# First batch of a channel-attention and FFN kernel: k loaded ahead of q, finer last parts of q, v transposed between the folds

## The chip, the cores and the metric

The kernel runs on one core of a Trainium2 chip. The metric is device time in microseconds, the median of several runs: 580.56 us for the kernel before, in 6 runs from 580.22 to 581.6. The engines are named as in the profile: PE is TensorE (PEld its weight loads), DVE VectorE, ACT ScalarE, POOL GpSimd, SP SyncE.

## The reference

q, k and v have the shape (4, 5824, 256) in float32: four batches of 5824 tokens with 256 channels. Attention is across channels, so its score matrix is 256 x 256 per batch, and its output goes through a feed-forward block with a product of two branches (d_ff = 1024):

```python
qn = q / (np.linalg.norm(q, axis=1, keepdims=True) + 1e-06)
kn = k / (np.linalg.norm(k, axis=1, keepdims=True) + 1e-06)
s = kn.transpose(0, 2, 1) @ qn / tau
a = np.exp(s - s.max(-1, keepdims=True))
a /= a.sum(-1, keepdims=True) + 1e-09
x = (v @ a).reshape(B * N, C)
out = ((x @ w1) * (x @ w2)) @ w3 @ w_out
```

tau is 1.0.

## The kernel before, in words

The attention matrix of a batch is folded into the weights: Wf = a @ [w1 w2] (256 x 2048), so that the tokens of v go directly to the two branches; w3 @ w_out is multiplied out once, into W_sb. The main loop (`emit_ab`, `emit_out`) then runs over 12 chunks of 512 tokens per batch and 8 blocks of 128 hidden channels: four 512-column matmuls of Wf against transposed v (line 419), ScalarE copies branch a (425), VectorE multiplies with branch b (428), and four 256-column matmuls with W_sb add to the output (452). While batch b is in its main loop, batch b+1's scores are computed in between, by a list with due times (`make_agenda`).

For batch 0 there is no earlier main loop to hide in. Its scores, softmax and folds are written out by hand, in program order, in lines 484 to 556; each engine takes its instructions in this order. A batch has 45 full tiles of 128 tokens and 64 tokens left over. They are loaded in six pieces, five of eight tiles and one (piece 5) of five tiles and the leftover. A piece of eight tiles is 512 KB in SBUF, one tile 64 KB; the loads convert float32 to bfloat16 and are all issued from POOL's queue, in program order (`load_piece`, lines 108 to 118, `cuts` splits a piece into several transfers). Buffers: five for q, so q's piece 5 takes the buffer of its piece 0, six for k, three for v.

What TensorE does with each tile of batch 0:

- `squares` (line 221): two 128-column matmuls that add the tile's squared columns into PSUM (`sqk` for k, `sqq` for q). The diagonal gives the norms.
- `products` (line 233), for q tiles, with the k tile of the same index: two 256-column matmuls that add to the score matrix G.
- `busy(n)` (line 209): n filler matmuls of 512 columns with no use for the result.

Issue order of the loads before: k0 (two halves), q0 (two halves), then k1 q1 k2 q2 k3 q3 k4 k5, q4 (two halves), q5 (leftover, then parts of two, two and one tiles), then w1 and w2 (first halves), half of v's piece 0, the second halves of w1, w2 and v's piece 0, v1, w3, w_out, v2. TensorE's order: squares of k0, then q0, then for pieces 1 to 3 squares of k, two fillers, squares and products of q; then squares of k4 and k5, k's norms, q4, q5.

The steps of the softmax (`soft_units`): `k_first` takes the diagonal of the k squares (DVE, 244); `k_row` spreads it by a float32 matmul (272) and makes 1/norm in four ScalarE activations (274 to 277); `q_first` (251) takes q's diagonal; `scaled_first` scales G (302), makes q's 1/norm (291 to 294) and the exponentials e, two on ScalarE (307); `first_folds` makes the column sums (323), 1/sum (329, 330) and folds 0 to 5. A fold is two 512-column matmuls (344) and an eviction to Wf, scaled by 1/sum, on ScalarE for even folds (351) and on VectorE for odd ones (353). Folds 6 and 7 come within the main loop. Before `first_folds` (line 555), TensorE transposes the first four tiles of v, 8 matmuls (132), and VectorE copies them out (136). The main loop's first matmul needs folds 0 and 1 and this part of v, its third folds 2 and 3.

Of the kernel before, what the change touches and what calls it, by code (L numbers as in the profile page):

```python
# [16 lines left out]
PIECE = 8  # L17
# [7 lines left out]
def kernel(  # L25
# [29 lines left out]
    LAST = NT - (NP_ - 1) * PIECE  # L55
# [44 lines left out]
    def new_piece(nm, n, pi):  # L100
        t = in_pool.tile([P, PIECE, C], BF16, tag=nm, name=f"{nm}_{n}_{pi}", bufs=IN_BUFS[nm])
        pieces[nm, n, pi] = t
        if pi == NP_ - 1:
            if nm != "v":
                nc.vector.memset(t[LEFT:, LAST, :], 0.0)
            nc.gpsimd.dma_start(out=t[:LEFT, LAST, :], in_=qk_main[nm, n][1])

    def load_part(nm, n, pi, lo, hi):
        nc.gpsimd.dma_start(  # L109
            out=pieces[nm, n, pi][:, lo:hi, :], in_=qk_main[nm, n][0][:, pi * PIECE + lo : pi * PIECE + hi, :]  # L110
        )

    def load_piece(nm, n, pi, cuts=()):

        new_piece(nm, n, pi)
        ends = [0, *cuts, LAST if pi == NP_ - 1 else PIECE]
        for lo, hi in zip(ends, ends[1:]):
            load_part(nm, n, pi, lo, hi)
# [3 lines left out]
    def new_vT(n):  # L122
        vTs[n] = (
            vT_pool.tile([P, NT - 1, CT, P], BF16, tag="vT", name=f"vT_{n}"),
            vT_pool.tile([P, CT, P + LEFT], BF16, tag="vTt", name=f"vTt_{n}"),
        )

    def pe_transpose(dst, src, tag, on_act):

        m = psum.tile([P, 8, P], BF16, tag=tag, name=f"tr_{nc.get_next_instruction_name()}", bufs={"ab": 4, "out": 3}[tag])  # L130
        for i, blk in enumerate(src):
            nc.tensor.transpose(m[:, i, :], blk, ident_b)
        if on_act:
            nc.scalar.copy(dst, m)
        else:
            nc.vector.tensor_copy(dst, m)

    def transpose_half_on_pe(n, pi, h, on_act):
        if pi == 0 and h == 0:
            new_vT(n)  # L140
        t = pieces["v", n, pi]
        i0 = 4 * h
        pe_transpose(
            vTs[n][0][:, pi * PIECE + i0 : pi * PIECE + i0 + 4, :, :].rearrange("p i c t -> p (i c) t"),
            [t[:, i0 + i, ct * P : (ct + 1) * P] for i in range(4) for ct in range(CT)],
            "out", on_act,
        )
# [57 lines left out]
    def busy(k):  # L205

        m = psum.tile([P, 512], F32, tag="ab", name=f"warm_{nc.get_next_instruction_name()}", bufs=4)
        for _ in range(k):
            nc.tensor.matmul(m, lhsT=warm[:, :P], rhs=warm, start=True, stop=True, skip_group_check=True)
# [3 lines left out]
    def squares(nm, pi, slots, end=False):  # L213

        if nm not in S:
            S[nm] = psum.tile([P, CT, P], F32, tag="out", name=f"sq{nm}_0", bufs=3)
        t = pieces[nm, 0, pi]
        for i in slots:
            for ct in range(CT):
                cs = slice(ct * P, (ct + 1) * P)  # L220
                nc.tensor.matmul(
                    S[nm][:, ct, :], lhsT=t[:, i, cs], rhs=t[:, i, cs],
                    start=(pi == 0 and i == 0 and ct == 0),
                    stop=(end and i == slots[-1] and ct == CT - 1), skip_group_check=True,
                )

    def products(pi, slots, end=False):
        if 0 not in G_tiles:
            G_tiles[0] = psum.tile([P, CT, C], F32, tag="G", name="G_0", bufs=1)
        qt, kt = pieces["q", 0, pi], pieces["k", 0, pi]  # L230
        for i in slots:
            for ct in range(CT):
                nc.tensor.matmul(
                    G_tiles[0][:, ct, :], lhsT=qt[:, i, ct * P : (ct + 1) * P], rhs=kt[:, i, :],
                    start=(pi == 0 and i == 0 and ct == 0),
                    stop=(end and i == slots[-1] and ct == CT - 1), skip_group_check=True,
                )

    def soft_units(n):
# [77 lines left out]
        def sum_mm(c2):  # L317
            if c2 == 0:
                st["sum"] = psum.tile([P, 512], F32, tag="out" if n == 0 else "ab", name=f"sum_{n}", bufs=3 if n == 0 else 4)
                Wf[n] = wf_pool.tile([P, CT, 2, F], BF16, tag="Wf", name=f"Wf_{n}")  # L320
            m = st["sum"]
            for c1 in range(CT):
                nc.tensor.matmul(
                    m[:, c1 : c1 + 1], lhsT=st["e"][:, c2, c1 * P : (c1 + 1) * P], rhs=ones_b,
                    start=(c1 == 0 and c2 == 0), stop=(c1 == CT - 1 and c2 == CT - 1), skip_group_check=True,
                )
            if c2 == CT - 1:
                rs = work.tile([P, CT], F32, tag="rs", name=f"rs_{n}", bufs=2)
                nc.vector.tensor_scalar_add(rs, m[:, :CT], 1e-9)
                nc.vector.reciprocal(rs, rs)  # L330
                st["rs"] = rs
# [2 lines left out]
            sum_mm(0)  # L334
            sum_mm(1)

        def fold_mm(i, c2, tag="ab"):
            h, rest = divmod(i, 4)
            w, c1 = divmod(rest, 2)
            if c2 == 0:  # L340
                st["fold", i] = psum.tile(
                    [P, 512], F32, tag=tag, name=f"fold_{n}_{i}", bufs={"ab": 4, "out": 3}[tag]
                )
            nc.tensor.matmul(  # L344
                st["fold", i], lhsT=st["e"][:, c2, c1 * P : (c1 + 1) * P], rhs=w12[:, c2, w, h * 512 : (h + 1) * 512],
                start=(c2 == 0), stop=(c2 == CT - 1),
            )
            if c2 == CT - 1:
                dst = Wf[n][:, c1, w, h * 512 : (h + 1) * 512]
                if i % 2 == 0:  # L350
                    nc.scalar.activation(out=dst, in_=st["fold", i], func=AF.Copy, scale=st["rs"][:, c1 : c1 + 1])  # L351
                else:
                    nc.vector.tensor_scalar_mul(dst, st["fold", i], st["rs"][:, c1 : c1 + 1])  # L353

        def fold(i, tag="ab"):
            fold_mm(i, 0, tag)
            fold_mm(i, 1, tag)

        def first_folds():
            sum_mm(0)  # L360
            fold_mm(0, 0)
            fold_mm(1, 0)
            sum_mm(1)
            fold_mm(0, 1)
            fold_mm(1, 1)
            fold(2)
            fold(3)
            fold(4, "out")
            fold(5, "out")

        if n == 0:
# [112 lines left out]
    half = PIECE // 2  # L484
    busy(14)
    load_piece("k", 0, 0, (half,))
    load_piece("q", 0, 0, (half,))
    masks.make_identity(nc, ident)
    nc.vector.tensor_copy(ident_b, ident)
    w3_wout = vT_pool.tile([P, (NT - 1) * C], BF16, tag="vT", name="w3_wout")  # L490
# [11 lines left out]
    w3r = moe_w3.rearrange("(jh jl) l -> jl jh l", jl=P)  # L502
    w1r = moe_w1.rearrange("(ch cl) f -> cl ch f", cl=P)
    w2r = moe_w2.rearrange("(ch cl) f -> cl ch f", cl=P)
    for pi in range(1, 4):
        load_piece("k", 0, pi)
        load_piece("q", 0, pi)
    load_piece("k", 0, 4)
    load_piece("k", 0, 5)
    soft0 = soft_units(0)  # L510
    whole = range(PIECE)
    lo, hi = range(half), range(half, PIECE)
    for sl in (lo, hi):
        squares("k", 0, sl)
        busy(2)
    for sl in (lo, hi):
        squares("q", 0, sl)
        products(0, sl)
    for pi in range(1, 4):
        squares("k", pi, whole)  # L520
        busy(2)
        squares("q", pi, whole)
        products(pi, whole)
    load_piece("q", 0, 4, (half,))
    load_piece("q", 0, 5, (2, 4))
    for h in range(2):
        hs = slice(h * F // 2, (h + 1) * F // 2)
        nc.gpsimd.dma_start(out=w12[:, :, 0, hs], in_=w1r[:, :, hs])
# [7 lines left out]
        nc.gpsimd.dma_start(out=w3_bf[:, js, :], in_=w3r[:, js, :])  # L536
    nc.gpsimd.dma_start(out=wout_sb, in_=moe_w_out.rearrange("(lh ll) c -> ll lh c", ll=P))
    load_piece("v", 0, 2)
    squares("k", 4, whole)
    squares("k", 5, range(LAST + 1), end=True)  # L540
    soft0[0]()
    busy(2)
    soft0[1]()
    for sl in (lo, hi):
        squares("q", 4, sl)
        products(4, sl)
    parts = [[LAST, 0, 1], [2, 3], [4]]
    for sl in parts:
        squares("q", 5, sl, end=sl is parts[-1])
        if sl is parts[-1]:  # L550
# [1 line left out]
        products(5, sl, end=sl is parts[-1])  # L552
    soft0[3]()
    busy(4)
    transpose_half_on_pe(0, 0, 0, False)
    soft0[4]()
    new_w3T()

# [116 lines left out]
```

## Time and profile before

| | |
|---|---|
| median of 6 runs | 580.56 us (580.22 to 581.6) |
| the profiled execution: its time | 580.45 us |
| its span, first to last instruction | 578.7 us |
| mean granted TensorE clock | 0.997 |
| busy PE / DVE / ACT / POOL | 98% / 65% / 59% / 11% of the span |
| first matmul of the main loop (line 419) starts at | 40.47 us |
| transfers, mean over the span | 129 GB/s |

Times in the profile are in us from the first instruction of the span. A timeline row is start, duration, engine, line, operation, output<-inputs, shape, count, and in brackets how long the engine had stood idle before it and what ended that. The chain of waits follows the work that ended last back to its start. A matmul row's duration has its way through the array in it; the rate of a run of matmuls is seen from the starts of the rows. The list of transfers gives the size of each issue and the time from its issue on POOL to its landing. A wait is put down to the releaser that came last.

### The profile page before, as it was taken

How to read it: one execution, taken by the hardware profiler on the slowest of the kernel's cores; microseconds unless marked ns; L12 is line 12 of the kernel's file. 1: busy time of each engine (PE TensorE's matmuls, PEld its weight loads, DVE VectorE, ACT ScalarE, POOL GpSimd, SP SyncE). 2: the span in 40 equal slices, each digit the busy share in tenths (PEclk: the TensorE clock that was granted, in tenths of full speed). 3: DMA queues.
4: the chain of work that ended last, by engine and by line, in shares of the span. 5: the costliest groups of instructions: out<-in, count | busy, mean ns of one | idle time of the engine just before them, and what ended most of it. 6: DMA issues, size and time to landing. Idle time of an engine off the chain costs nothing.

```text
span 578.7 us, 10224 instructions
## 1 busy us (share of the span) xinstructions
PE 565.2 (98%) x3826; PEld 360.9 (62%) x3834; DVE 376.5 (65%) x601; ACT 341.4 (59%) x628; POOL 64.1 (11%) x142
## 2 busy tenths in 40 slices
PE   7799999999999999999999999999999999999996
PEld 4665676766656566666666666666665666556664
DVE  0047545888877567788766667778876656565564
ACT  0046535777765576777765476767665554454453
POOL 5240021110000202001000112001100000000000
PEclk9999999999999999999999999999999999999998
DMA  8999989773543899555652699754563335311011
GB/s 163 211 207 198 172 154 206 161 169 77 120 100 109 128 228 176 111 110 125 128 127 74 144 199 174 169 113 87 146 132 87 83 78 145 83 40 72 37 72 56
DMA packets 66113, 74.85 MB, mean 129 GB/s; under 512 B 45840, under 2 KB 49808, under 8 KB 66064
## 3 DMA queue, kind: packets, MB, share of 16 engines
q0 software_dynamic: 15376, 39.46, 39.8%
q1 hardware_dynamic: 50544, 34.61, 20.3%
q8 instruction: 30, 0.49, 0.3%
q14 instruction: 19, 0.16, 0.1%
q10 hardware_dynamic: 144, 0.13, 0.1%
HBM read 78.91 MB, written 23.86 MB: 178 GB/s over the span
## 4 chain that ended last, share of the span: by engine, by line
PE 89%; DMA 6%; DVE 1%; ACT 1%; issue 1%; POOL 1%; ACTq 0%; POOLq 0%
PE o L452 27%; PE a L419 26%; PE b L419 26%; PE G L188 5%; DMA q<-in_q_dram 4%; PE fold L344 2%; PE w L570 1%; DMA v<-in_v_dram 1%; ACT as L425 1%; DVE abs L428 1%; POOL k L109 0%; DVE osb L473 0%; PE row L272 0%; PE ss L283 0%; ACT e L307 0%
## 5 line engine op out<-in xcount | busy, mean ns | idle before, releaser
L428 DVE TENSOR_TENSOR abs<-as,b 128x512 bf16<-128x512 bf16 x352 | 240.5, 685 | 147.9 <-ACT as L425 137.0
L425 ACT CAST as<-a 128x512 bf16<-128x512 f32 (+1 forms) x384 | 215.4, 562 | 172.7 <-DVE abs L428 83.7
L452 PE MATMUL o<-W_sb,abs 128*128 128x256 bf16 x1440 | 218.1, 273 | 0.5 <-ACT osb L472 0.4
L419 PEld LDWEIGHTS <-Wf 128*128 128x128 bf16 x1536 | 148.9, 98 | 98.1 <-issue 1.7
L419 PE MATMUL a<-vT,Wf 128*128 128x512 bf16 x704 | 209.4, 379 | 0.4
L419 PE MATMUL b<-vT,Wf 128*128 128x512 bf16 x704 | 209.3, 379 | 0.1
L452 PEld LDWEIGHTS <-abs 128*128 128x128 bf16 x1440 | 140.7, 98 | 86.2 <-issue 0.6
L197 DVE TENSOR_TENSOR acc<-acc,sq 128x1024 f32<-128x1024 f32 x66 | 80.4, 1219 | 0.1
L411 POOL COPY gate_t<-abs 1x1 bf16<-1x1 bf16 x39 | 10.3, 265 | 394.9 <-DVE abs L428 386.7
L188 PE MATMUL G<-k,q 128*128 128x256 bf16 x276 | 49.7, 273 | 0.0
L185 ACT ACTIVATE sq<-q 128x512 f32<-128x512 bf16 x66 | 41.8, 633 | 0.0
L185 ACT ACTIVATE sq<-k 128x512 f32<-128x512 bf16 x66 | 41.6, 630 | 0.0
L473 DVE COPY osb<-o 128x512 f32<-128x512 f32 x44 | 30.1, 684 | 0.4 <-PE o L452 0.4
L188 PEld LDWEIGHTS <-q 128*128 128x128 bf16 x276 | 27.0, 98 | 3.3 <-issue 0.2
L472 ACT COPY osb<-o 128x512 f32<-128x512 f32 x44 | 25.7, 585 | 3.8 <-PE o L452 1.7
L274 ACT ACTIVATE kr<-row 128x256 f32<-128x256 f32 x4 | 1.5, 383 | 31.1 <-PE row L272 31.1
L109 POOL DMA_DIRECT2D q<-in_q_dram x28 | 15.0, 538 | 13.8 <-DMA k<-in_k_dram 5.2
L344 PE MATMUL fold<-w,e 128*128 128x512 bf16 x61 | 16.0, 378 | 0.1
L351 ACT ACTIVATE Wf<-fold,rs 128x512 bf16<-128x512 f32 x16 | 10.8, 687 | 8.8 <-PE fold L344 4.7
L109 POOL DMA_DIRECT2D v<-in_v_dram x25 | 13.5, 540 | 6.6 <-issue 4.9
L109 POOL DMA_DIRECT2D k<-in_k_dram x25 | 13.8, 551 | 3.4 <-DMA k<-in_k_dram 1.9
L353 DVE TENSOR_SCALAR Wf<-fold,rs 128x512 bf16<-128x512 f32 x16 | 11.8, 748 | 2.1 <-PE fold L344 1.8
(103 smaller groups left out, 196.8 us busy)
## 6 DMA issues: line engine op xcount, KB each, us to landing
out_dram<-osb SPq DMA_DIRECT2D x44, 512.0 KB, 3.0
k<-in_k_dram POOLq DMA_DIRECT2D x19, 512.0 KB, 9.2
v<-in_v_dram POOLq DMA_DIRECT2D x19, 512.0 KB, 5.2
q<-in_q_dram POOLq DMA_DIRECT2D x18, 512.0 KB, 6.4
w_wout<-in_moe_w_dram POOLq DMA_DIRECT2D x2, 1024.0 KB, 16.2
k<-in_k_dram POOLq DMA_DIRECT2D x4, 320.0 KB, 6.5
v<-in_v_dram POOLq DMA_DIRECT2D x4, 320.0 KB, 5.0
q<-in_q_dram POOLq DMA_DIRECT2D x4, 256.0 KB, 10.6
```

The source lines that it names most:

```text
L109: nc.gpsimd.dma_start(out=pieces[nm, n, pi][:, lo:hi, :], in_=qk_main[nm, n][0][:, pi * PIECE + lo : pi * PIECE + hi, :])
L185: nc.scalar.activation(out=dst[:, :, part, :], in_=src[:, o : o + 2, :], func=AF.Square)
L188: nc.tensor.matmul(G[:, ct, :], lhsT=qt[:, i, ct * P : (ct + 1) * P], rhs=kt[:, i, :], start=(pr == 0 and part == 0 and ct == 0), stop=(pr ...
L197: nc.vector.tensor_add(accs[n], accs[n], sqs[0])
L344: nc.tensor.matmul(st["fold", i], lhsT=st["e"][:, c2, c1 * P : (c1 + 1) * P], rhs=w12[:, c2, w, h * 512 : (h + 1) * 512], start=(c2 == 0), ...
L353: nc.vector.tensor_scalar_mul(dst, st["fold", i], st["rs"][:, c1 : c1 + 1])
L419: nc.tensor.matmul(t[:, :n], lhsT=Wf[b][:, ct, w, j * P : (j + 1) * P], rhs=rhs_of(b, c, ct), start=(ct == 0), stop=(ct == CT - 1),)
L425: nc.scalar.copy(a_sb[:, :n], tiles[0][:, :n])
L428: nc.vector.tensor_mul(ab, a_sb, tiles[1])
L452: nc.tensor.matmul(tl[s // 2][:, s % 2, :], lhsT=lhsT, rhs=W_sb[:, j, :], start=(j == 0 and s % 2 == 0), stop=(j == FT - 1 and (s % 2 == 1 ...
L472: nc.scalar.copy(o[:, 0:2, :], tl[0])
L473: nc.vector.tensor_copy(o[:, 2:4, :], tl[1])
```

## The change

All edits are in batch 0's start. The loads of q0 and k1 to k3 change places: k0 (two halves), k1, k2, k3, q0 (one transfer now), k4, q1, k5, q2, q3, then q4 in four parts of two tiles, and q5 as leftover and parts of one, two, one and one tiles. The order of squares and products follows: squares of k1, k2 and k3 with four fillers behind each; q0 and squares of k4; q1 and squares of k5; k's diagonal; first half of q2; k's row matmul; second half of q2; q3; q4 by two tiles; q5 as leftover and tile 0, tiles 1 and 2, tile 3, tile 4. The transposes of v's first four tiles move from ahead of the sums to behind fold 2. Fold 3 is evicted by ScalarE instead of VectorE, fold 4 by VectorE instead of ScalarE.

```diff
-        def fold_mm(i, c2, tag="ab"):
+        def fold_mm(i, c2, tag="ab", on_act=None):
...
-                if i % 2 == 0:
+                if on_act if on_act is not None else i % 2 == 0:
...
-        def fold(i, tag="ab"):
+        def fold(i, tag="ab", on_act=None):
             fold_mm(i, 0, tag)
-            fold_mm(i, 1, tag)
+            fold_mm(i, 1, tag, i % 2 == 0 if on_act is None else on_act)
...
             fold(2)
-            fold(3)
-            fold(4, "out")
+            transpose_half_on_pe(0, 0, 0, False)
+            fold(3, on_act=True)
+            fold(4, "out", on_act=False)
             fold(5, "out")
...
     load_piece("k", 0, 0, (half,))
-    load_piece("q", 0, 0, (half,))
+    load_piece("k", 0, 1)
...
-    for pi in range(1, 4):
-        load_piece("k", 0, pi)
-        load_piece("q", 0, pi)
-    load_piece("k", 0, 4)
-    load_piece("k", 0, 5)
+    for nm, pi in [("k", 2), ("k", 3), ("q", 0), ("k", 4), ("q", 1), ("k", 5), ("q", 2), ("q", 3)]:
+        load_piece(nm, 0, pi)
+    load_piece("q", 0, 4, (2, 4, 6))
...
-    for sl in (lo, hi):
-        squares("q", 0, sl)
-        products(0, sl)
     for pi in range(1, 4):
         squares("k", pi, whole)
-        busy(2)
+        busy(4)
+    for pi in range(2):
         squares("q", pi, whole)
         products(pi, whole)
-    load_piece("q", 0, 4, (half,))
-    load_piece("q", 0, 5, (2, 4))
+        squares("k", pi + 4, whole if pi == 0 else range(LAST + 1), end=pi == 1)
+    load_piece("q", 0, 5, (1, 3, 4))
...
-    squares("k", 4, whole)
-    squares("k", 5, range(LAST + 1), end=True)
     soft0[0]()
-    busy(2)
+    squares("q", 2, lo)
+    products(2, lo)
     soft0[1]()
-    for sl in (lo, hi):
-        squares("q", 4, sl)
-        products(4, sl)
-    parts = [[LAST, 0, 1], [2, 3], [4]]
+    squares("q", 2, hi)
+    products(2, hi)
+    squares("q", 3, whole)
+    products(3, whole)
+    for i in range(0, PIECE, 2):
+        squares("q", 4, [i, i + 1])
+        products(4, [i, i + 1])
+    parts = [[LAST, 0], [1, 2], [3], [4]]
...
     soft0[3]()
     busy(4)
-    transpose_half_on_pe(0, 0, 0, False)
     soft0[4]()
```

## The prediction

> **What bounds the kernel now.** I read the first two parts of the page, then the chain of waits in order of time for the first 45 us (all edits lie there), then TensorE's timeline for that stretch, and last the transfers.
>
> ```profile
> span 578.7 us, 10224 instructions
> PE 565.2 (98%) x3826; PEld 360.9 (62%) x3834; DVE 376.5 (65%) x601; ACT 341.4 (59%) x628; POOL 64.1 (11%) x142
> ```
>
> TensorE has work all the time once batch 0's main loop runs, so whatever delays or advances the first matmul of that loop (line 419, at 40.47 us) shifts everything behind it. No wait of TensorE on a transfer appears after that point.
>
> ```profile
> 14.42 15.69 DMA q<-in_q_dram
> 30.11 0.29 issue
> 30.40 6.88 DMA v<-in_v_dram
> 37.28 0.05 issue
> 37.33 0.62 PE tr_I-495_496 L132 x8
> 37.94 0.03 PE sum L323 x2
> ```
>
> Start, duration, what. The first 37 us of the chain are loads; its last step is half a piece of v, which TensorE waits for before it transposes. But this chain names only what came last, by 0.05 us. TensorE's own rows show what is nearly as late (start, duration, line, output<-inputs, count, idle before):
>
> ```profile
> 14.18 1.07 PE L221 MATMUL sqq<-q 128*128 128x128 bf16 x16 [0.92 <-DMA q<-in_q_dram]
> 15.08 1.91 PE L233 MATMUL G<-k,q 128*128 128x256 bf16 x16
> 16.82 1.06 PE L221 MATMUL sqk<-k 128*128 128x128 bf16 x16
> ...
> 20.41 1.07 PE L221 MATMUL sqq<-q 128*128 128x128 bf16 x16 [2.31 <-DMA q<-in_q_dram]
> ...
> 28.91 0.84 PE L221 MATMUL sqk<-k 128*128 128x128 bf16 x12 [0.50 <-DMA k<-in_k_dram]
> 29.59 0.38 PE L209 MATMUL warm_I-405_406<-warm 128*128 128x512 bf16 x1
> 30.27 0.70 PE L272 MATMUL row<-dk,ones_pp 128*128 128x256 f32 x2 [0.30 <-DVE dk L244]
> 30.80 0.61 PE L221 MATMUL sqq<-q 128*128 128x128 bf16 x8
> ...
> 35.20 0.38 PE L233 MATMUL G<-k,q 128*128 128x256 bf16 x2
> 35.42 1.03 PE L209 MATMUL warm_I-487_488<-warm 128*128 128x512 bf16 x3
> 37.33 0.62 PE L132 MATMUL tr_I-495_496<-ident_b,v 128*128 128x128 bf16 x8 [0.88 <-DMA v<-in_v_dram]
> ...
> 40.47 0.59 PE L419 MATMUL a<-vT,Wf 128*128 128x512 bf16 x2
> ```
>
> From 30.80 on no wait stands between the rows: TensorE, not the loads, sets the end of the products, P = 35.42 (the start of the next row). ScalarE's two exponentials run from 36.82 to 37.73, and the sums start at 37.78. So the softmax behind P would have held the folds back to about the same time as v.
>
> **Prices.** Starts give the rates: squares of eight q tiles 15.08-14.18 = 0.90, their products 16.82-15.08 = 1.74, together 2.64 a piece, 0.33 a tile (check: 14 tiles from 30.80 to 35.42 = 4.62). Squares of eight k tiles 0.90, of k's last six 0.68. The row matmul 30.80-30.27 = 0.53. A 512-column matmul 0.216.
>
> Landing times are issue plus time to landing in the transfers view, asked for at each issue. By KB landed so far they are: 1024 at 9.3, 1536 at 11.7, 2048 at 14.1, 2560 at 16.6, 3072 at 20.4, 3584 at 22.2, 4096 at 24.7, 4608 at 27.1, 4960 at 28.9, 5216 at 30.1, 5472 at 31.7, 5824 (the last q) at 33.5. That is 2.45 us for a 512 KB piece, 0.31 a tile, but for one step: 3072 came 3.8 us behind 2560. In that step lies a fetch of instructions; here is the queue list for the stretch 18 to 19 us (packets, MB, share of 16 engines):
>
> ```profile
> q0 software_dynamic: 62, 0.19, 97.0%
> q8 instruction: 1, 0.02, 5.9%
> ```
>
> 5.9% of 16 engines for 1 us is 0.94 us of one engine. Of the sixteen landing counts that the trace has for that load, fifteen came by 19.1 and the last at 20.36, so one engine was late; the last counts of the later loads stay about 0.7 us behind the others. (The Trainium skill, "Runtime: NRT & Kernel Launch", Instruction fetch mechanics, says that crossing a 16 KiB block costs a tail-bump, "mostly hidden". The row speaks against that for a load that something waits for; by the page the sum below would be that of rival B.)
>
> **The change, step by step.**
>
> *Load order.* The bytes are the same, so I put the new order on the same curve: k1 at 9.3, k2 11.7, k3 14.1, q0 16.6, k4 20.4 (19.1 if the fetch falls later), q1 22.2, k5 23.9, q2 (4448 KB, 69% of the way from 24.68 to 27.13) 26.37, q3 28.9, q4 in four parts 29.5 to 31.7, q5 to 33.5. No load before q2 is held up by its issue: POOL's waits in the trace fit eight transfers in flight (each issue waits for the eighth before it), which puts q2's issue behind k1's landing at 9.3.
>
> *TensorE up to q2.* k1 to k3 take 0.90 plus four fillers of 0.216 each; their six extra fillers (1.3 us) lie inside the 2.45 between landings and cost nothing. q0 16.6 to 19.25; k4 20.4 to 21.3; q1 22.2 to 24.85; k5 to 25.5. Then it waits for q2 until 26.37, plus 0.05 (14.13 to 14.18 in the row above): 26.42. What is late is a load, with TensorE 0.9 us behind it.
>
> *TensorE from q2.* Here lies the loss. With k ahead, every tile that arrives now takes 0.33 of TensorE against 0.31 of transfer, and whole pieces q2 and q3 start a piece behind. Left to do: 30 tiles (8+8+8+6) at 0.33 = 9.90, and the row matmul 0.53: P = 26.42+10.43 = 36.85. It reaches q4 at 32.0 (landed 29.5 to 31.7) and the first part of q5 at 34.6 (landed 31.9); the last tile, landed at 33.5, is begun at 36.5. So the finer parts of q4 and q5 remove no wait, since none is left there. Before, 14 tiles and no k were left at 30.80, and TensorE had filled its idle time earlier with q. Step: 36.85-35.42 = +1.43.
>
> *The cuts.* q4 is issued in four instead of two, q5's main part in four instead of three, q0 in one instead of two: two more issues on POOL at 0.55 = 1.1 us, beside POOL's waits for landings. What is queued behind them there are w1, w2 and v. Their issues come later (the first w1 waits for 5216 KB: 30.4 instead of 27.96), but about 600 KB, 2.9 us, still stand in the queues then, and the shortest time to first packet is that of the first load (issued 1.24, packets from 2.6): no gap. Bounds: nothing to the 2.4 us by which the loads run ahead of TensorE; I take nothing, by the rows of the 128, 128 and 64 KB parts of q5 that landed at 32.5, 33.1 and 33.5, in step with their bytes. (The Trainium skill, "DMA: Bandwidth & Descriptors", Bandwidth, advises batches of 1 MiB and calls those under 64 KB descriptor-dominated; its fit charges 2.0 us per transfer. By it two more would add an estimated 4 us. The rows just named show no such charge with transfers queued behind each other.)
>
> *v between the folds.* From P: first exponential done at 37.28 = P+1.86 (half of the pair), second P+2.31. TensorE: sum and two folds' first halves from P+1.91 to 2.37, second sum and four matmuls to 3.26, eight transposes 0.45 to 3.71, six fold matmuls 1.30 to P+5.01. Before: 40.47-35.42 = P+5.05. Gain 0.04. v lands at 37.3, wanted at P+3.26 = 40.1: its wait is gone, and the softmax is late instead. Evictions, with 1/sum ready near P+3.05 (before 0.49 later): ScalarE folds 0, 2, 3 until P+5.05 (0.65 each), VectorE fold 1, v (0.69), folds 4, 5 until P+6.25. The loop's first matmul needs folds 0, 1 and v (P+4.6); its third at P+5.45 needs folds 2 and 3; the first product on VectorE, P+6.25, follows fold 5 directly. Bounds: -0.05 to +0.69 if one eviction slips by one; I take -0.04.
>
> *Sum.* +1.43-0.04 = +1.39 on the profiled execution's 580.45 (span 578.7, 1.75 around it): 581.84. The median of the six runs, 580.56, lies 0.11 above that execution; between, 581.9.
>
> **Rivals.**
> A, the forecast: q alone is TensorE's to finish, 581.9. Chance 0.60.
> B, the fetch falls behind q2's landing, or is hidden: q2 at 25.7, P = 36.2, +0.7: 581.2. For it: fillers and order change when TensorE crosses a block. Against: the same count of matmuls has run by q0's end (126) as by 17.5 us before. 0.17.
> C, the other side: the end is set by the last load. One tile behind 33.5 is P = 33.9, and v at 37.3 just serves transposes at P+3.26: -1.5, 579.0, faster. It decides if TensorE needs under 0.25 a tile from 26.4 to 33.9; no row has under 0.33. 0.05.
> D, small parts and eight in flight starve the queues, or an eviction slips: over 582.4, up to 583.5. For it: only 600 KB in flight at w1's issue. Against: 2.4 us of slack. 0.10.
> E, nothing comes of it: 580.5. The landing order could differ from the issue order, so that q2 comes early, at 25.0. The rows show landings in order. 0.08.
>
> **Numbers.** About 0.2% (1.16 us) is what a measurement of this kernel can tell from no change; the bounds are 579.4 and 581.7. A lies just over the upper one: 0.42 slower, 0.18 same. B 0.02 and 0.15, D 0.10 slower, E same, C faster: faster 0.05, same 0.41, slower 0.54. Range 580.5 to 583.0: it takes in A, B, most of D and half of E.
>
> **What would show it.** After: a wait for q before q2's squares (about 26.4) and none for q from there to the last product; that product near 36.9; last q landed near 33.5; sums before the transposes, with no wait for v; first main matmul near 41.9; granted clock 1.00 throughout (before it was 1.00 even in 15 to 20 us, with 3.10 us busy and a pause of 2.31). Wrong if TensorE waits for q4 or q5 (then C or D), if q2 starts before 25.5 (B or E), or if the main loop waits for an eviction or w.

## The result, and the profile after

The changed kernel takes 582.17 us (median of 20 runs, 581.68 to 583.42) against 580.81 us for the kernel before (40 runs, 580.15 to 582.11). The ratio is 1.0023, 95% interval 1.0017 to 1.0029: slower by 1.36 us. The forecast was 581.9, slower, in a range of 580.5 to 583.0.

The profiled execution took 582.57 us. Two lines of its page:

```profile
span 580.7 us, 10236 instructions
PE 568.1 (98%) x3833; PEld 362.2 (62%) x3838; DVE 376.7 (65%) x601; ACT 341.5 (59%) x628; POOL 65.2 (11%) x144
```

TensorE's timeline at the places that the prediction named (start, duration, line, output<-inputs, count, idle before; the loop's first matmul, line 419 before, is line 420 here):

```profile
19.84 1.07 PE L221 MATMUL sqk<-k 128*128 128x128 bf16 x16 [0.47 <-DMA k<-in_k_dram]
22.21 1.47 PE L221 MATMUL sqq<-q 128*128 128x128 bf16 x16 [1.30 <-DMA q<-in_q_dram]
23.48 3.20 PE L233 MATMUL G<-k,q 128*128 128x256 bf16 x16
26.52 0.83 PE L221 MATMUL sqk<-k 128*128 128x128 bf16 x12
27.19 0.61 PE L221 MATMUL sqq<-q 128*128 128x128 bf16 x8
...
37.52 1.03 PE L209 MATMUL warm_I-491_492<-warm 128*128 128x512 bf16 x3
39.49 0.20 PE L323 MATMUL sum<-ones_b,e 128*128 128x1 bf16 x2 [0.94 <-ACT e L307]
...
40.89 0.61 PE L132 MATMUL tr_I-520_521<-ident_b,v 128*128 128x128 bf16 x8
...
42.63 0.59 PE L420 MATMUL a<-vT,Wf 128*128 128x512 bf16 x2
```

Three things are to be seen. From q2's squares (27.19) to the last product (ending at 37.52) no wait stands between the rows, as forecast. The wait for v is gone, and the wait for the exponentials (0.94) stands in its place. And q1 has an unforeseen length: its squares start at 22.21 and k5's squares, which follow its products, at 26.52, 4.31 us for work that took 2.64 before. The busy time by stretch shows why (busy us and count of PE, PEld, DVE, ACT, POOL, then TensorE's granted clock, DMA share, GB/s):

```profile
19.28:22.70 3.42, 1.65 (x26) 1.39 (x26) 0.17 (x1) 0.00 (x0) 0.78 (x2) 1.00 1.10 211
22.70:26.11 3.41, 3.41 (x24) 2.61 (x22) 0.00 (x0) 0.00 (x0) 1.36 (x3) 0.50 1.06 213
```

For 3.41 us the clock was granted at half. The forecast wait for q2 is not seen in this execution: q1's slow work swallows it. So the main loop starts at 42.63 instead of 40.47, 2.16 us later, of which the order of the work explains only a part. The experiments below split it.

### The profile page after: what moved, and what is told of

It reads as the page before. It is cut to its first block, busy times and chain, and to the rows that moved or that the text cites. A ratio compares the mean times of both kernels' runs of the same rounds, so it can differ in the third digit from the quotient of the medians.

```text
span 580.7 us, 10236 instructions
## 1 busy us (share of the span) xinstructions
PE 568.1 (98%) x3833; PEld 362.2 (62%) x3838; DVE 376.7 (65%) x601; ACT 341.5 (59%) x628; POOL 65.2 (11%) x144
## 4 chain that ended last, share of the span: by engine, by line
PE 91%; DMA 3%; ACT 1%; DVE 1%; issue 1%; POOL 1%; ACTq 0%; POOLq 0%
PE o L453 27%; PE a L420 26%; PE b L420 26%; PE G L188 5%; DMA q<-in_q_dram 3%; PE fold L344 2%; PE G L233 2%; PE w L569 1%; ACT as L426 1%; DVE abs L429 1%; PE sqq L221 1%; POOL k L109 1%; PE row L272 0%; DVE osb L474 0%; ACT e L307 0%
## 5 line engine op out<-in xcount | busy, mean ns | idle before, releaser
L188 PE MATMUL G<-k,q 128*128 128x256 bf16 x276 | 49.8, 273 | 0.0
L233 PE MATMUL G<-k,q 128*128 128x256 bf16 x92 | 13.3, 292 | 0.0
```

Source lines behind the costliest of these rows:

```text
L188: nc.tensor.matmul(G[:, ct, :], lhsT=qt[:, i, ct * P : (ct + 1) * P], rhs=kt[:, i, :], start=(pr == 0 and part == 0 and ct == 0), stop=(pr ...
L233: nc.tensor.matmul(G_tiles[0][:, ct, :], lhsT=qt[:, i, ct * P : (ct + 1) * P], rhs=kt[:, i, :], start=(pi == 0 and i == 0 and ct == 0), st ...
```

## The experiments

Each kernel was timed in five rounds beside the kernel before on the same chip. In the texts, P is the end of the last product (the start of the filler row behind it), and "loop" the start of the first matmul of the main loop, both from the profile. Before: P 35.42, loop 40.47.

Three theories were to be told apart. A: TensorE's own work behind q2's landing sets P, and a stretch at half clock comes on top where it strikes. C: the last loads of q set P. H: the half clock is the whole loss.

**1. The fold edits alone** (before, with the edits of `fold_mm`, `fold` and `first_folds`).

```diff
             fold(2)
-            fold(3)
-            fold(4, "out")
+            transpose_half_on_pe(0, 0, 0, False)
+            fold(3, on_act=True)
+            fold(4, "out", on_act=False)
...
     busy(4)
-    transpose_half_on_pe(0, 0, 0, False)
```

Expected:

> The kernel before with the fold edits alone (v's transposes behind fold 2, folds 3 and 4 with swapped engines); loads and TensorE's order as before. Theory A (the loss is TensorE's q work behind q2's landing, and the folds are worth 0.04 us): within 0.2 us of before, first main-loop matmul at about 40.4 us in the profile. Rival F (the wait for v was a real loss and moving the transposes gains it): 0.5 to 0.9 us faster, that matmul at 39.6 to 40.0. Rival G (evictions slip): slower by 0.3 to 0.7.

Measured: 581.41 against 581.0 us, ratio 1.0007 (0.9998 to 1.0016), within what can be told from no change. P is 35.44 and the loop starts at 40.87, 0.40 later than before. Of that, 0.31 is one VectorE instruction that took 0.48 us here and 0.17 before (told of at the end); without it the edits cost 0.09. So moving the transposes gains nothing (rival F falls). No eviction is waited for either, so by the profile rival G falls too; the time alone would still allow it. That the wait for v cost nothing before does not follow: the next experiment shows what it cost, and that the new place of the transposes costs about as much.

**2. The loads alone** (the changed kernel, with the folds and the transposes where they were before: the diff of experiment 1 the other way round).

Expected:

> The changed kernel with the folds as before: only the load order, the cuts and TensorE's order are new. Theory A: as slow as the whole change, 1.0 to 1.6 us over before; last product at 36.9 (granted clock 1.00) or up to 37.7 (with one window at half clock). Rival G (the fold edits cost the time): no more than 0.3 us over before.

Measured: 582.0 against 581.0, ratio 1.0018 (1.0008 to 1.0027). The load order carries the loss. Its timeline behind the products:

```profile
36.81 1.03 PE L209 MATMUL warm_I-491_492<-warm 128*128 128x512 bf16 x4
37.92 0.45 PEld L132 LDWEIGHTS <-v 128*128 128x128 bf16 x8 [0.58 <-DMA v<-in_v_dram]
37.93 0.62 PE L132 MATMUL tr_I-499_500<-ident_b,v 128*128 128x128 bf16 x8
38.77 0.20 PE L323 MATMUL sum<-ones_b,e 128*128 128x1 bf16 x2 [0.23 <-ACT e L307]
...
41.48 0.59 PE L419 MATMUL a<-vT,Wf 128*128 128x512 bf16 x2
```

P is 36.81 with the granted clock at 1.00. The transposes start at 37.93, as soon as v has landed (their weight loads wait for it), and still lie in the time in which TensorE would otherwise wait for the exponentials; the loop starts 41.48-36.81 = 4.67 behind P. Before it was 5.05: there v landed later behind P, and its wait cost 0.38. With the fold edits it is 42.63-37.52 = 5.11. So in the late order the old place of the transposes was free, and the new one costs 0.44 us of TensorE by these profiles. The times of the two kernels don't tell that apart.

**3. The pause ahead of q1 filled.** The changed kernel, and:

```diff
         squares("k", pi + 4, whole if pi == 0 else range(LAST + 1), end=pi == 1)
+        if pi == 0:
+            busy(5)
```

Expected:

> The changed kernel with five more filler matmuls behind k4's squares, in the pause of 1.3 us ahead of q1, so that no stretch of 3.4 us is idle for over half. Theory A with the half clock as an extra of some executions: granted clock 1.00 throughout, q2's squares at 26.4, last product at 36.9, first main matmul at 41.9; the time 0.2 to 0.7 us below the changed kernel and still 0.9 to 1.2 us over before. Rival H (the half clock is all of the loss): level with before, within 0.3 us.

Measured: 581.88 against 581.0, ratio 1.0016 (1.0007 to 1.0025).

```profile
20.97 1.24 PE L209 MATMUL warm_I-282_283<-warm 128*128 128x512 bf16 x5
22.23 1.07 PE L221 MATMUL sqq<-q 128*128 128x128 bf16 x16
...
26.45 0.62 PE L221 MATMUL sqq<-q 128*128 128x128 bf16 x8 [0.74 <-DMA q<-in_q_dram]
...
36.79 1.03 PE L209 MATMUL warm_I-498_499<-warm 128*128 128x512 bf16 x4
...
41.91 0.59 PE L420 MATMUL a<-vT,Wf 128*128 128x512 bf16 x2
```

The clock is 1.00, q2 starts at 26.45, P is 36.79 and the loop starts at 41.91. The kernel is still slower than before, so H falls: the half clock is not the whole loss. In the profiles it is 27.19-26.45 = 0.74 of the 2.16 us.

**4. Filler in the tail.** The changed kernel, and:

```diff
     products(3, whole)
+    busy(4)
     for i in range(0, PIECE, 2):
         squares("q", 4, [i, i + 1])
```

Expected:

> The changed kernel with four filler matmuls (0.86 us of TensorE) between q3 and q4, a place where the loads are ahead by the profile. Theory A (TensorE's work sets the end): 0.86 us slower than the changed kernel, some 2.2 over before. Rival C (the last loads set it): the filler hides in a wait, no change against the changed kernel (within 0.2 us).

Measured: 582.94 against 581.0, ratio 1.0032 (1.002 to 1.0043).

```profile
32.18 1.03 PE L209 MATMUL warm_I-420_421<-warm 128*128 128x512 bf16 x4
...
42.78 0.59 PE L420 MATMUL a<-vT,Wf 128*128 128x512 bf16 x2
```

The loop starts 42.78-41.91 = 0.87 behind that of experiment 3, whose clock was also 1.00: all 0.86 us of filler are paid. No load is waited for between q3 and P. C falls for this order.

**5. The coarse end.** The changed kernel, with q4 and q5 cut and worked off as before:

```diff
-    load_piece("q", 0, 4, (2, 4, 6))
+    load_piece("q", 0, 4, (half,))
...
-    load_piece("q", 0, 5, (1, 3, 4))
+    load_piece("q", 0, 5, (2, 4))
...
-    for i in range(0, PIECE, 2):
-        squares("q", 4, [i, i + 1])
-        products(4, [i, i + 1])
-    parts = [[LAST, 0], [1, 2], [3], [4]]
+    for sl in (lo, hi):
+        squares("q", 4, sl)
+        products(4, sl)
+    parts = [[LAST, 0, 1], [2, 3], [4]]
```

Expected:

> The changed kernel with q4 and q5 cut, and worked off, as before (q4 in halves; q5 in the leftover and parts of two, two and one tiles). Theory A (TensorE is behind the loads from q2 on): the finer cuts are worth nothing, so the time stays within 0.3 us of the changed kernel, 1.0 to 1.5 us over before, last product at 36.8 where the granted clock is 1.00. Rival C (the last loads set the end): 0.5 to 1 us slower than the changed kernel, with a wait for q ahead of q4 or q5.

Measured: 582.07 against 580.53, ratio 1.0023 (1.0015 to 1.0032), the changed kernel's own ratio. P is 36.62, and in a second profile of the changed kernel (experiment 9) it is 36.62 too. The finer parts of q4 and q5 are worth nothing here.

**6. Finer q1, q2 and q3.** The kernel of experiment 5, with these pieces loaded and worked off in parts of two tiles:

```diff
-        load_piece(nm, 0, pi)
+        load_piece(nm, 0, pi, (2, 4, 6) if nm == "q" and pi > 0 else ())
...
+    pairs = [[i, i + 1] for i in range(0, PIECE, 2)]
     for pi in range(2):
-        squares("q", pi, whole)
-        products(pi, whole)
+        for sl in pairs if pi else [whole]:
+            squares("q", pi, sl)
+            products(pi, sl)
```

(q2 and q3 likewise.) Expected:

> The kernel of the coarse-end run, but with q1, q2 and q3 loaded and worked off in parts of two tiles. Theory A, with the whole pieces q1 to q3 as what leaves TensorE idle and then behind: it goes on from k4 at about 21 us with short waits, last product at 35.1 to 35.3 (1.6 us earlier than 36.8), first main matmul near 40.3, 1.3 to 1.8 us faster than the coarse-end run and 0 to 0.5 us faster than before. Rival I (k ahead leaves too much q work whatever the cuts): last product stays above 36.3.

Measured: 580.52 against 580.53, ratio 1.0 (0.9991 to 1.0009): 1.55 us less than experiment 5 beside it, and level with before.

```profile
20.46 1.06 PE L221 MATMUL sqk<-k 128*128 128x128 bf16 x16
21.36 0.39 PE L221 MATMUL sqq<-q 128*128 128x128 bf16 x4
...
35.70 1.03 PE L209 MATMUL warm_I-497_498<-warm 128*128 128x512 bf16 x4
```

q1 starts directly behind k4's squares, at 21.36 instead of 22.06 to 22.23, and P is 35.70 (35.1 to 35.3 was expected; in this execution k1 landed 1.2 us late, and the clock was at half from 11.07 to 14.48). So what made the changed kernel late is that q1 to q3 came whole: TensorE idled until eight tiles were there and then had all eight in front of it. Rival I falls. The loop starts at 40.82 in this profile, where 40.3 was expected, 0.35 behind before, 0.28 of it in P.

**7. v's first half ahead of the weights.** Before, with one transfer moved:

```diff
+    new_piece("v", 0, 0)
+    load_part("v", 0, 0, 0, half)
     for h in range(2):
...
-        if h == 0:
-            new_piece("v", 0, 0)
-        load_part("v", 0, 0, h * half, (h + 1) * half)
+    load_part("v", 0, 0, half, PIECE)
```

Expected:

> The kernel before with one transfer moved: the first half of v's piece 0 is issued ahead of w1 and w2's first halves; transposes and folds as before. If v's late landing (37.3) cost the kernel before what the run with new loads and old folds shows (transposes inside the softmax's wait, main loop 4.67 us behind the last product instead of 5.05): first main matmul at 40.1, 0.3 to 0.5 us faster than before. Rival: w1 and w2 land 1.3 us later (36.0 and 37.3) and the folds wait for them: no gain, or slower by up to 0.5.

Measured: 580.38 against 580.53, ratio 1.0 (0.9991 to 1.0009). A miss: no gain is seen. In its profile the transposes run at 36.44 without a wait, but the sums wait for the exponentials until 37.90, 2.32 behind P (35.58), where 1.96 is usual (38.77-36.81 in experiment 2). The 0.35 are again one VectorE instruction, 0.52 instead of 0.17 us. The loop starts at 40.60. No fold waits for a weight load, so the rival's reason is not seen. The interval reaches about 0.5 us each way, so these times can't exclude the 0.3 to 0.5 that were expected either.

**8. Finer q1 to q3 and v first** (6 and 7 together, folds and transposes as before).

Expected:

> The kernel with q1 to q3 in parts of two tiles, with v's first half issued ahead of w1 and w2 and the folds and transposes as before. Both pieces of theory A together: last product at 35.2, first main matmul 4.67 behind it at 39.9, 0.5 to 0.9 us faster than before. If the fold edits of the change are worth keeping (rival), it is no faster than the run with fine q1 to q3 alone.

Measured: 580.25 against 580.53, ratio 0.9995 (0.9986 to 1.0004). P is 35.53, the loop starts at 40.20, 4.67 behind P as expected, but P missed its 35.2: here TensorE waited 0.31 us for q4's second half. Once q1 to q3 are fine, the coarse q4 does count. The gain of 0.3 us is not clear of no change, and neither is the 0.27 against experiment 6 beside it.

**9. The changed kernel and the filled pause again,** side by side.

Expected of the changed kernel:

> The changed kernel once more, on the same chip and beside the same runs as the next one. By theory A with the half clock as an extra of some executions, its fastest runs are those of the run with the filled pause (some 1.2 us over the fastest of before), its spread reaches 0.8 us higher, and its median is 0.1 to 0.5 us higher. If no execution of the filled kernel differs from these, the half clock is too rare to move the median. The profile may or may not show a stretch at half clock.

Expected of the filled pause:

> The changed kernel with five fillers behind k4's squares, once more, beside the changed kernel on the same chip: granted clock 1.00 up to the last product, last product at 36.8, median 0.1 to 0.5 us below the changed kernel's and 0.9 to 1.3 over before.

Measured: 582.55 (7 runs, 581.58 to 583.05) and 581.9 (8 runs, 581.55 to 583.15) against 580.72; ratios 1.0025 (1.0014 to 1.0037) and 1.0023 (1.0013 to 1.0033). The medians lie 0.65 apart, a little more than expected, but the fastest and the slowest runs of the two are alike and the intervals of their ratios overlap. This profile of the changed kernel has no stretch at half clock:

```profile
26.28 0.62 PE L221 MATMUL sqq<-q 128*128 128x128 bf16 x8 [0.73 <-DMA q<-in_q_dram]
...
36.62 1.03 PE L209 MATMUL warm_I-491_492<-warm 128*128 128x512 bf16 x4
...
41.73 0.59 PE L420 MATMUL a<-vT,Wf 128*128 128x512 bf16 x2
```

The loop starts only 1.26 behind before, and 0.90 ahead of the first profile; experiment 3 had put the half clock at 0.74. But its time was 582.55, as long as that of the first profiled execution. The rest came much later, in batch 1 (start, duration, line, output<-inputs, count, idle before):

```profile
205.76 0.38 PE L188 MATMUL G<-k,q 128*128 128x256 bf16 x2 [0.81 <-DMA k<-in_k_dram]
```

In the first profile, the same matmuls wait for nothing. The wait stands in five of the thirteen profiles, with 0.35 to 0.96 us (experiments 1 and 5, both profiles of the filled pause, and this one). It does not go by how late the loop starts: experiment 4, whose loop is 2.31 late, has none, and experiment 1, 0.40 late, has 0.41. What brings it is not known. It is one of the things that spread single executions, and it hides the half clock: what that adds to the median is not settled by these runs.

**10. A load order made from the sums.** Before, with k just ahead of q to the end, finer pieces where TensorE would wait, and v's first half ahead of w1 and w2; the core of its diff:

```diff
-    for pi in range(1, 4):
-        load_piece("k", 0, pi)
-        load_piece("q", 0, pi)
-    load_piece("k", 0, 4)
+    load_piece("k", 0, 1)
+    load_piece("q", 0, 1)
+    load_piece("k", 0, 2)
+    load_piece("q", 0, 2, (half,))
+    load_piece("k", 0, 3)
     load_piece("k", 0, 5)
+    new_piece("k", 0, 4)
+    load_part("k", 0, 4, 0, half)
+    load_piece("q", 0, 3, (half,))
+    load_part("k", 0, 4, half, PIECE)
...
+    load_piece("q", 0, 4, (2, 4, 6))
     load_piece("q", 0, 5, (2, 4))
```

Expected:

> A load order made by theory A's sums, from the kernel before: k0 q0 k1 q1 k2, q2 in halves, k3 k5, half of k4, q3 in halves, the rest of k4, q4 in quarters, q5 (leftover, two, two, one), with v's first half ahead of w1 and w2, folds and transposes as before, and TensorE's order to match. k stays just ahead of q, so neither is left over. Theory A: last product at 34.8 (0.6 ahead of before), first main matmul 4.67 behind it at 39.5, 0.7 to 1.2 us faster than before. Rival: the last loads or the weights w1, w2 (landing 36.0 and 37.3) take over as the bound, and it is no faster than the run with fine q1 to q3 and v first, 0.3 us under before.

Measured: 580.13 against 580.72, ratio 0.999 (0.9981 to 0.9998): faster than before, by 0.6 us.

```profile
35.07 1.03 PE L209 MATMUL warm_I-484_485<-warm 128*128 128x512 bf16 x4
...
39.31 1.04 PE L344 MATMUL fold<-w,e 128*128 128x512 bf16 x4 [0.26 <-DMA w<-in_moe_w_dram]
40.19 0.59 PE L419 MATMUL a<-vT,Wf 128*128 128x512 bf16 x2
```

P is 35.07 (34.8 expected), but the loop starts 5.12 behind it: folds 4 and 5 now wait for a weight load. The rival was right to that extent: the loop starts 0.28 ahead of before instead of 1.0, and the gain stays under the 0.7 to 1.2 that were expected.

## Why the prediction was right, and where it wasn't

- **What bounds the start.** Right. The loop's start moves the end with it: TensorE's main loop runs 2.16 us later throughout batch 0 in the profile after, 0.40 and 1.00 in experiments 1 and 2, the same at each block up to batch 1's wait.
- **Load curve.** Right. q2 was put at 26.37 and its squares at 26.42; experiment 3 has 26.45, the changed kernel's second profile 26.28. The landing order and the rates held. In the first profile the forecast wait ahead of q2 is missing, because of the clock (below).
- **The fetch of instructions.** Right in place: the list of transfers has one at 17.63 (18.34 before), ahead of q2. Rival B didn't come.
- **TensorE's work from q2.** Right: 10.43 forecast, 36.79-26.45 = 10.34 measured. The difference is the row matmul, put at 0.53 from a row that had begun behind a wait; between other matmuls it is 28.94-28.51 = 0.43. P was to be 36.85 and is 36.79. The reason given for the loss, k ahead of q, was only half of it: with k as far ahead and q1 to q3 in small parts, P is 35.70 and 35.53 (experiments 6 and 8), close to the 35.42 before. What counts is that the pieces came whole.
- **The cuts.** Right: nothing (experiments 4 and 5).
- **v between the folds.** The size failed, and its reasoning. The gain of 0.04 was a cost: 5.11 to 5.12 behind P in the changed kernel, against 5.05. The first exponential takes 0.52 of the pair's 0.91, not half. More important, I took it that the softmax held the folds to about the same time as v, and so compared with the place that v's late landing forced before. But the first sum needs only the first exponential, which was done at 36.82+0.51 = 37.33, while the transposes behind v held the sum until 37.78. The new load order alone gains this back (4.67 instead of 5.05 behind P). The sum of the change is not touched by that, but its parts are: the loads cost 1.01 (41.48-40.47), the fold edits 0.43 on top (41.91-41.48), together 1.44 against 1.39 forecast.
- **The granted clock.** Wrong. I said 1.00 throughout, because a pause of 2.31 us had not lowered it. What decided was not the longest pause (1.47 us here) but, as far as thirteen profiles show, how busy TensorE was within a window of 3.41 us (last section): the stretch of the kernel before that I leaned on lies mostly in a window that was busy for 62%. Where it strikes, q1 takes 4.31 instead of 2.64 us, and after what the wait for q2 swallows, 0.74 are left at q2. My D named no such thing.
- **The number.** 581.9 against 582.17. The profiled execution has 582.57-580.45 = 2.12 over that of before, 1.39 from the forecast steps and the rest from the clock; the medians differ by 1.36. That these agree so well with 1.39 is partly luck, since the median also has the wait in batch 1 in it, and perhaps some half clock. The 0.27 by which 581.9 is too low is nearly all the kernel before: its median was 580.56 when I forecast and is 580.81 beside the changed one.

## What to carry to other kernels

Load order and work order are one plan: when one operand comes early and the other then comes in whole pieces, the engine idles until a piece is complete, and has that much more work left at the end. Put each piece on the curve of landings, add the engine's work behind it, and cut the pieces at which the engine first waits and then falls behind; parts of the last pieces help only if the engine is waiting there. And before moving work out of a wait, ask whether the wait will still be there after the other edits: a place inside a wait is free.

## What the runs showed of the hardware

**The clock goes by windows.** The stretches at half clock were 3.41 us long and began a whole number of 3.41 us steps after the clock had first risen to full. In the windows between the start and P in thirteen profiles, three were followed by half clock: TensorE was busy in them for 48% (the changed kernel, row above: 1.65 of 3.42), 19% (experiment 6) and 43% (experiment 7):

```profile
17.38:20.80 3.42, 1.48 (x21) 0.99 (x19) 0.00 (x0) 0.00 (x0) 0.42 (x1) 1.00 1.07 216
20.80:24.21 3.41, 3.41 (x20) 2.41 (x18) 0.00 (x0) 0.00 (x0) 0.67 (x2) 0.50 1.07 215
```

The least busy window without that effect had 52% (experiment 5). The steps lie differently in each execution (the clock first rose at 5.63 us in the changed kernel's first profile and at 5.98 in its second), so the same kernel is struck in one and not in another. The Trainium skill, "TensorE: Matmul & The Clock Gate", Part 1, gives a free-running window of 3413 ns, which agrees, and says that the clock falls after an idle window. Its section "Why this matters for your kernels" advises against pauses over about 3 us. Here a window that was 48% busy, with no pause over 1.47 us (the changed kernel), was followed by half clock; the measurement decides.

**A VectorE instruction that ends with a DMA issue on POOL.** An instruction of q's 1/norm in the softmax (line 293, 128x2) took 0.17 us in nine of the thirteen profiles. Here are its rows in experiments 1 and 7:

```profile
36.44 0.48 DVE L293 TENSOR_SCALAR r<-r 128x2 f32<-128x2 f32 x1 [0.17 <-ACT r L292]
```

```profile
36.58 0.52 DVE L293 TENSOR_SCALAR r<-r 128x2 f32<-128x2 f32 x1 [0.17 <-ACT r L292]
```

POOL was issuing w_out's load then, from 36.07 to 36.96 and from 36.18 to 37.11, and both instructions end when the issue does (36.92 and 37.10). The other two cases are like it: 0.27 us in the second profile of the filled pause (it ends at 37.88, an issue at 37.92) and 0.19 in experiment 10 (both end at 36.26). Before, the issue had begun only 0.11 us ahead of the instruction, and it took 0.17. This fits the lock on the port that VectorE and GpSimd share, of which the Trainium skill tells in "SBUF — State Buffer", section "Who interferes with whom": whoever comes first keeps it for the whole instruction. By that alone the instruction before should have been held too, unless the issue takes the port only some time after it begins. This was not tested by moving the issue.
